# Attention and token routing in one kernel: the planner's keys get a seeded random addition, and its account of durations and landings is set anew

## The chip, the cores and the metric

The kernel runs on one core of one Trainium2 chip. The metric is device time in microseconds (us); less is better. A core has TensorE (PE in the profile; its weight loads are PEld), VectorE (DVE), ScalarE (ACT), GpSimd (POOL) and SyncE (SP), which here only issues DMA transfers. Each engine takes its instructions strictly in the order in which the program holds them. So the order of each queue is part of the program, and it is all that this change alters.

## The reference

Two stages, one after the other, all in float32:

```python
# attention: q, k, v of shape (8 batches, 8 heads, 576 tokens, 64)
q_rot, k_rot = rotate(q), rotate(k)                 # rotary embedding
scores = (1 / sqrt(64)) * q_rot @ k_rot.T
attn = exp(scores - max(scores)); attn /= sum(attn) + 1e-9
x = (attn @ v).transpose(0, 2, 1, 3).reshape(8, 576, 512)
# routing, for each batch: the 128 tokens with the highest x . w_gate
xe = x[b, top_idx]
ye = max(xe @ w1, 0) @ w2                           # 512 -> 1024 -> 512
x[b, top_idx] += sigmoid(score)[:, None] * ye
```

## The kernel before, in words

**Tiling.** Two heads of a batch form a pair; there are 32 pairs, four to a batch. A pair's queries are cut into nine units: units 0 to 7 are 128 queries of one head, unit 8 holds the last 64 of both heads.

**A pair, step by step** (lines of the kernel before). SP loads k, q and v from DRAM (L438). POOL rotates k and q (L456). PE turns them (L518), ACT and POOL split each into a high and a low part (L529 to L533, for small pieces L538 to L542). PE makes the scores (L610): twelve matmuls for two units at once (units 0 and 1, 2 and 3, 4 and 5, 6 and 7), six for unit 8; this is a score group. Each unit's scores fill two of the eight PSUM banks, so one score group of two units holds four. DVE takes the negative maximum of each unit (L627), ACT the exponential and the sum (L631); when ACT has read a unit, its banks are free. DVE then transposes the exponentials in blocks of 32x32 into the tiles `pt` (L645), and SP moves rows of `pt` from partitions to partitions (L658), six transfers for part 0 (units 0 to 3; tile pt_96) and six for part 1 (units 4 to 8; tile pt_97). The first four of six wait for the transposes alone; the last two overwrite what the first two read, and so also wait for these to land. Then PE multiplies by v (L687, the value product; 36 matmuls in the program, 72 records in the trace; it holds two banks), ACT or DVE copies the result out (L334, L336), PE turns it back and takes the gate's dot products (L731, L732; one bank), and DVE scales it (L742 to L754). After every second pair SP stores half the rows of the batch (L794, L796).

**Routing.** When a batch has its four pairs, DVE counts ranks and selects 128 tokens (L809 to L899), POOL gathers them by an indirect DMA (L906), PE runs the two layers (L924 to L971, the products are L952), and POOL scatters the rows back (L991). The weights are loaded, split and stored during the first pairs (L1014 to L1018), through two staging tiles, with POOL taking part in each of the sixteen pieces.

**What sets the order.** The kernel's code records operations (`op`) with the engine, a duration, a key, the operations that must come first, and the PSUM banks. `Order.run` then plays the whole program in its own account of time: whenever an engine is free, it takes the ready operation with the lowest key, with exceptions for score groups (`urgent`), for PE's change of tile shape (`TURN`) and for operations that would block an urgent one. Keys are due times: pair `pi` owns the stretch from `20000 * pi` on. An operation's account holds two numbers, how long its engine is taken and after how long its result is there. SP's transfers are put one after the other at 3.6 ns per KB. Where PE would idle, a filler matmul (L345) is put in, if PE was busy less than `warm` of the last stretch of the account. The list that comes out is the program; on the chip nothing is reordered.

## Time and profile before

| | us |
|---|---|
| three runs | 674.64, 681.92, 679.69 |
| median | 679.69 |
| the profiled execution, as a run | 676.31 |
| its span, first to last instruction | 674.6 |
| PE, DVE, POOL, ACT busy | 585.3, 543.9, 424.4, 361.9 |
| PE filler matmuls (L345) | 35.2 |
| granted TensorE clock, mean | 0.976 |

The profiled execution lies 1.7 us above its own span and 3.4 us under the median of the three runs. Busy times are sums over the whole span; a stage can have another limit than the mean. A wait is idle time of the engine just before an instruction, put down to whatever came last.

### The profile page before, as it was taken

Reading aid. Unit: us, or ns where it says so; the run is one execution under the profiler, and the core shown is the slowest. Engines: PE = TensorE matmul, PEld = TensorE weight load, DVE = VectorE, ACT = ScalarE, POOL = GpSimd, SP = SyncE. Lnnn points to the kernel's source line nnn. Section 1 sums busy time; section 2 is a strip of 40 time slices with the busy share of each in tenths; the row PEclk is TensorE's granted clock in tenths of the full one; section 3 lists DMA queues with packets and bytes.
Section 4 is the critical chain, followed back from the end, with each engine's and each line's share of the span. In section 5 each row is a group of like instructions: output and inputs, shape, how many; then the busy total and the mean of one; then the engine's idle time right before and its main releaser. Section 6 shows DMA issues by size and latency. Waiting matters only on the chain.

```text
span 674.6 us, 20156 instructions
## 1 busy us (share of the span) xinstructions
PE 585.3 (87%) x7828; PEld 492.9 (73%) x7828; DVE 543.9 (81%) x1348; ACT 361.9 (54%) x960; POOL 424.4 (63%) x489
## 2 busy tenths in 40 slices
PE   3787788688999988899899897989888898999997
PEld 2666667577877777788777776768777787777875
DVE  6777678868899987998889888898889878997451
ACT  2566656436666655466655556375555456554111
POOL 2989889955877565677694498475794487510101
PEclk9889999989999999899999999999999899989999
DMA  5677888748776766766785779757685776646400
GB/s 203 153 204 205 254 230 225 178 117 231 200 216 175 211 191 205 194 190 180 202 233 126 213 195 240 179 149 189 177 232 143 208 192 182 168 107 164 133 17 32
DMA packets 45951, 122.14 MB, mean 181 GB/s; under 512 B 8864, under 2 KB 18080, under 8 KB 45856
## 3 DMA queue, kind: packets, MB, share of 16 engines
q1 hardware_dynamic: 44432, 116.17, 63.6%
q0 software_dynamic: 1280, 4.20, 2.1%
q8 instruction: 62, 1.02, 0.7%
q10 hardware_dynamic: 144, 0.49, 0.2%
q14 instruction: 33, 0.27, 0.1%
HBM read 45.58 MB, written 11.53 MB: 85 GB/s over the span
## 4 chain that ended last, share of the span: by engine, by line
PE 39%; DVE 19%; DMA 16%; issue 8%; POOL 7%; ACT 7%; SPq 3%; POOLq 0%; DVEq 0%; ACTq 0%
PE ps L687 16%; DMA pt<-pt 10%; DVE pt L645 8%; PE ps L610 7%; DVE nm L627 6%; PE ps L952 6%; ACT pab L631 4%; PE ps L518 3%; SPq L658 3%; DMA xe<-w_dram 3%; PE ps L731 2%; DMA xe<-out_dram,idx 2%; PE ps L345 2%; POOL w L1018 1%; POOL m L456 1%
## 5 line engine op out<-in xcount | busy, mean ns | idle before, releaser
L631 ACT ACTIVATE pab<-ps,nm 128x576 f32<-128x576 f32 x256 | 187.1, 738 | 116.2 <-DVE nm L627 115.9
L627 DVE TENSOR_REDUCE nm<-ps 128x1 f32<-128x576 f32 x288 | 200.8, 737 | 20.2 <-PE ps L610 19.1
L645 DVE STREAM_TRANSPOSE pt<-pab 128x576 f32<-128x576 f32 x256 | 185.2, 751 | 36.0 <-PE ps L687 17.8
L687 PE MATMUL ps<-pt,vt 64*64 64x128 f32 (+1 forms) x4608 | 189.6, 300 | 25.2 <-DMA pt<-pt 8.8
L687 PEld LDWEIGHTS ps<-pt,vt 64*64 64x64 f32 x4608 | 164.7, 139 | 46.1 <-ACT pab L631 14.8
L610 PE MATMUL ps<-kh,qh 64*128 64x288 f32 (+1 forms) x576 | 88.0, 343 | 6.1 <-ACT pab L631 5.0
L456 POOL TENSOR_TENSOR rk<-k_in,m 128x512 f32<-128x512 f32 (+1 forms) x62 | 52.7, 867 | 58.8 <-PE ps L518 58.5
L610 PEld LDWEIGHTS ps<-kh,qh 64*128 64x128 f32 (+1 forms) x576 | 52.9, 192 | 34.7 <-issue 17.8
L610 PE MATMUL ps<-kh,ql 64*128 64x288 f32 (+1 forms) x576 | 72.0, 298 | 0.9 <-POOL ql L533 0.9
L456 POOL TENSOR_TENSOR rq<-q_in,m 64x64 f32<-64x64 f32 (+1 forms) x93 | 58.0, 637 | 23.4 <-PE ps L518 18.0
L533 POOL TENSOR_TENSOR kl<-xf,kh 128x512 fp32r<-128x512 f32 x31 | 39.6, 1278 | 52.3 <-ACT xf L531 38.8
L610 PE MATMUL ps<-kl,qh 64*128 64x288 f32 (+1 forms) x576 | 71.9, 297 | 0.0
L731 PE MATMUL ps<-ident,ot 128*128 128x128 f32 x160 | 47.2, 308 | 25.9 <-ACT pab L631 24.5
L334 ACT COPY ot<-ps 64x64 f32<-64x64 f32 (+1 forms) x114 | 29.0, 282 | 74.5 <-PE ps L687 73.5
L456 POOL TENSOR_TENSOR m<-k_in,tabs 128x320 f32<-128x320 f32 x62 | 52.7, 867 | 14.0 <-DVE rq L456 12.5
L731 PEld LDWEIGHTS ps<-ident,ot 128*128 128x128 f32 x160 | 30.5, 190 | 35.3 <-ACT pab L631 29.9
L610 PEld LDWEIGHTS ps<-kh,ql 64*128 64x128 f32 (+1 forms) x576 | 54.7, 191 | 1.1 <-POOL ql L533 1.1
L610 PEld LDWEIGHTS ps<-kl,qh 64*128 64x128 f32 (+1 forms) x576 | 55.0, 191 | 0.0
L952 PE MATMUL ps<-w,ht 128*128 128x512 f32 x192 | 52.7, 410 | 0.6 <-ACT pab L631 0.3
L952 PE MATMUL ps<-w,xt 128*128 128x512 f32 x192 | 52.1, 412 | 0.0
L631 ACT ACTIVATION_READ_ACCUMULATOR pab<-ps,nm 128x1 f32 x256 | 51.1, 199 | 0.0
L732 PEld LDWEIGHTS ps<-wg,ot 128*128 128x128 f32 x320 | 49.1, 209 | 1.1
(105 smaller groups left out, 923.1 us busy)
## 6 DMA issues: line engine op xcount, KB each, us to landing
pt<-pt SPq DMA_DIRECT2D x192, 180.0 KB, 3.7
pt<-pt SPq DMA_DIRECT2D x192, 144.0 KB, 3.6
vt<-v_dram SPq DMA_DIRECT2D x32, 576.0 KB, 4.9
k_in<-k_dram SPq DMA_DIRECT2D x32, 320.0 KB, 5.1
q_in<-q_dram SPq DMA_DIRECT2D x32, 288.0 KB, 4.9
out_dram<-x SPq DMA_DIRECT2D x16, 512.0 KB, 3.4
xe<-w_dram SPq DMA_DIRECT2D x8, 256.0 KB, 3.8
row<-w_dram SPq DMA_DIRECT2D x8, 256.0 KB, 4.1
```

What stands on the lines that cost most here:

```text
L334: nc.scalar.copy(out, in_)
L456: lambda: e.tensor_tensor(out, in0, in1, op=alu), key, after)
L518: nc.tensor.transpose(bank_of(b)[:, i * P:i * P + P], r.tile[:, t].rearrange("p h d -> p (h d)"), ident)
L533: d = op({"POOL": pool(n)}, lambda: nc.gpsimd.tensor_tensor(lo, xf.tile, hi.bitcast(F32), op=ALU.subtract), key, [c, y] + lu.before)
L610: nc.tensor.matmul(bank_of(bs[i])[:, n, 0:HALF], lt, rt, start=first, stop=last)
L627: lambda: nc.vector.tensor_reduce(nm.tile[:, u:u + 1], bank_of(b)[:, :, 0:HALF], axis=AX.XY, op=ALU.max, negate=True),
L631: lambda: nc.scalar.activation(dst.rearrange("p (n c) -> p n c", n=2), bank_of(b)[:, :, 0:HALF], AF.Exp, bias=nm.tile[:, u:u + 1], scale=1 ...
L645: lambda: nc.vector.transpose(pt[c].tile[:, 0:2, :, to, :].rearrange("p w m j -> p m w j"), src.rearrange("p (m w j) -> p m w j", w=2, j=32)),
L687: nc.tensor.matmul(bank_of(acc)[64 * h:64 * h + 64, g, :].rearrange("p (w c) -> p w c", w=2)[:, :, c0:c0 + n], vt.tile[gp_, h, m % 2 * NT ...
L731: nc.tensor.transpose(bank_of(b)[:, i * P:i * P + P], cols, ident)
L732: nc.tensor.matmul(bank_of(b)[:, 400 + 2 * i:402 + 2 * i], cols, wg[:, j, :], start=True, stop=True)
L952: nc.tensor.matmul(bank_of(bank), lhs.tile[:, a, c * P:c * P + P], w[w_][:, c, fs], start=(c == 0 and i == 0), stop=(c == n - 1 and i == 2))
```

## The change

It alters what the planner is told and the keys, and no operation. (1) Every key in a stretch of 20000 whose entry in `SEEDS` is not 0 gets a normally distributed addition with a standard deviation of 400, drawn from a generator with that seed. (2) Durations in the account: POOL's operations, the SP loads and stores (a load's result is now there after 4200 instead of 2000), the value product of part 1 (326 for each step instead of 283), the turning back with the gate (295 for each turned block instead of 169), the splits of the gate's scores. (3) Landings: a transfer that is issued while an earlier load has not landed is taken to land only with that load, or 2500 after it, whichever is sooner. (4) `warm` goes from 0.75 to 0.78.

```diff
@@ -1,3 +1,4 @@
+import random
 from contextlib import ExitStack
 
 import concourse.bass as bass
@@ -20,9 +21,14 @@
 EPS = 1e-9
 
 
-KEY = dict(landing=2500, warm=0.75, warm0=20000, warm1=1000000, dummy=430, dcols=256, ahead=8500, lag=13000, rem=400, value=4300, rows=3000, load=22300, rotate=115700, half=2500,
+KEY = dict(landing=2500, warm=0.78, warm0=20000, warm1=1000000, dummy=430, dcols=256, ahead=8500, lag=13000, rem=400, value=4300, rows=3000, load=22300, rotate=115700, half=2500,
            gate=11700, route=58400, count=35500, select=12400, turn=17500, step=7600, kstep=2700, hold=3,
            patience=900, over=300, near=-300, swap=6000, vsplit=9, vstep=0, recip=6000, pool_lo=1, esplit=2, s_pairs=(0, 1, 2, 3), t_banks=(2, 3, 4, 5, 6, 7), t_most=4)
+
+
+SEEDS = (395, 668, 0, 37, 0, 386, 92, 332, 986, 288, 947, 432, 0, 151, 886, 935, 438, 375, 753, 239, 325, 690, 0, 636, 130, 791,
+         968, 161, 387, 940, 0, 423, 25)
+NOISE = 400.0
 
 
 class Bank:
@@ -44,7 +50,7 @@
     SEM = 45.0
     BLOCK, FETCH = 256, 3900.0
     WINDOW, FALL, RISE = 3413.0, 0.58, 0.88
-    PER_KB = 3.6
+    PER_KB, BEHIND = 3.6, 2500.0
 
 
     TURN = {(0, 1): 97.0, (1, 0): 92.0, (0, 2): 187.0, (2, 0): 89.0, (1, 2): 187.0, (2, 1): 97.0,
@@ -93,7 +99,7 @@
                 takes -= step / (2 if slow else 1)
                 at_ += step
             return at_ - begin
-        count, fetched, moving = 0, 0.0, 0.0
+        count, fetched, moving, landing = 0, 0.0, 0.0, 0.0
         waiting = {e: [] for e in names}
         idle = [0.0] * (2 * self.pairs)
         held = {}
@@ -214,6 +220,10 @@
                     if e == "SP":
                         moving = max(moving, begin + takes) + self.PER_KB * o.size
                         begin += max(0.0, moving - begin - takes)
+                        if o.mode:
+                            landing = begin + lasts
+                        elif begin < landing:
+                            lasts = max(lasts, min(landing - begin, self.BEHIND))
                     for b in o.banks:
                         if b.slot is None:
                             b.slot = take(b.kind)
@@ -321,13 +331,13 @@
         return {"ACT": act(n), "DVE": dve(n)}
 
     def pool(n):
-        return (60 + 2.38 * n, 60 + 2.38 * n)
+        return (max(388, 60 + 2.29 * n), max(410, 100 + 2.29 * n))
 
     def pe(ns):
         return {"PE": (ns, ns + 165)}
 
     T32, T32R, M288, M512 = 109.0, 84.0, 132.5, 248.0
-    LOAD, STORE = {"SP": (500, 2000)}, {"SP": (600, 2000)}
+    LOAD, STORE = {"SP": (520, 4200)}, {"SP": (620, 2700)}
 
     def copy(e, out, in_):
         if e == "ACT":
@@ -436,7 +446,7 @@
         for i, (n, src, use) in enumerate((("k", k, kin), ("q", q, qin), ("v", v, vt))):
             if n in names:
                 o = op(LOAD, lambda src=src, use=use: nc.sync.dma_start(use.tile, src[b, j]), key + i,
-                       use.before + list(after), size=320)
+                       use.before + list(after), mode=1, size=320)
                 use.by(o)
                 got[n].append(o)
 
@@ -693,7 +703,7 @@
             o = None
             for m0 in range(0, NB // 2, KEY["vsplit"]):
                 m1 = min(m0 + KEY["vsplit"], NB // 2)
-                o = op(pe((m1 - m0) * (228 + 55 * c)), lambda m0=m0, m1=m1: products(m0, m1), key,
+                o = op(pe((m1 - m0) * (216 + 110 * c)), lambda m0=m0, m1=m1: products(m0, m1), key,
                        moved[c] + got["v"] + [o], acc, mode=1, size=16 * (m1 - m0))
                 key += KEY["vstep"]
             for use in (vt, pt[c]):
@@ -735,7 +745,7 @@
                 xrows[b_, j // 2] = xs.next()
             x = xrows[b_, j // 2]
             cs = slice(j % 2 * P, j % 2 * P + P)
-            f = op(pe((2 + c) * (T32 + 60)), turns, key, [es] + const_ready, b, size=6 * (2 + c))
+            f = op(pe((2 + c) * 295), turns, key, [es] + const_ready, b, size=6 * (2 + c))
             ot.by(f)
 
             def rows_of():
@@ -863,7 +873,7 @@
             nc.gpsimd.tensor_copy(cols[1], r1.tile)
             nc.gpsimd.tensor_tensor(cols[2], r1.tile, cols[1], op=ALU.subtract)
 
-        o = op({"POOL": (500, 500)}, parts, key, [s] + tk.before + r1.before)
+        o = op({"POOL": (1050, 1050)}, parts, key, [s] + tk.before + r1.before)
         sc.by(o), tk.by(o), r1.by(o)
         return tk, o
 
@@ -1011,8 +1021,8 @@
             st = stages.next()
             stage = st.tile
             key = at(1 + i // 4, 0.2 * (i % 4))
-            l = op(LOAD, lambda src=src, stage=stage: nc.sync.dma_start(stage, src), key,
-                   st.before + [anchors[i % 4 - 5]], size=256)
+            l = op({"SP": (520, 2900)}, lambda src=src, stage=stage: nc.sync.dma_start(stage, src), key,
+                   st.before + [anchors[i % 4 - 5]], mode=1, size=256)
             c = op({"ACT": act(DM)}, lambda hi=hi, stage=stage: nc.scalar.copy(hi, stage), key + 3000, [l])
             d = op({"POOL": pool(DM)},
                    lambda hi=hi, lo=lo, stage=stage: nc.gpsimd.tensor_tensor(
@@ -1052,6 +1062,11 @@
                 for l in held:
                     l(anchors[-KEY["hold"]:-KEY["hold"] + 1])
                 held.clear()
+    draws = [random.Random(1000 * i + n) for i, n in enumerate(SEEDS)]
+    for o in order.ops:
+        i = min(max(int(o.key // PAIR), 0), len(SEEDS) - 1)
+        if SEEDS[i]:
+            o.key += draws[i].gauss(0, NOISE)
     for _, _, o, e in order.run():
         o.fn(e) if len(o.engines) > 1 else o.fn()
```

The program that comes out has the same instructions but for one more filler matmul (67 instead of 66 in the program, two records each in the trace) and one copy that passes from DVE to ACT. The queues' order differs widely.

In the following rows kh, kl, qh, ql are the split keys and queries of a score group, ot the output of a value product, pt and vt the exponentials and v. The change's line numbers are higher by 10 (L620 is L610 of before).

**PE, around the value product of part 0 of pair 19.** Before:

```order
L687 MATMUL ps<-pt_96,vt_90 64x2x64 x36
L610 MATMUL ps<-kh_81,qh_85 128x288 x4
L610 MATMUL ps<-kl_83,qh_85 128x288 x4
L610 MATMUL ps<-kh_81,ql_87 128x288 x4
L610 MATMUL ps<-kh_81,qh_85 128x288 x4
L610 MATMUL ps<-kl_83,qh_85 128x288 x4
L610 MATMUL ps<-kh_81,ql_87 128x288 x4
L731 MATMUL ps<-ident,ot_98 128x128
```

With the change:

```order
L697 MATMUL ps<-pt_96,vt_90 64x2x64 x36
L528 MATMUL ps<-ident,rk_79 128x128 x4
L620 MATMUL ps<-kh_81,qh_85 128x288 x4
L620 MATMUL ps<-kl_83,qh_85 128x288 x4
L620 MATMUL ps<-kh_81,ql_87 128x288 x4
L741 MATMUL ps<-ident,ot_98 128x128
```

Two score groups stood back to back ahead of the turning back; now one stands there, and the turning of the next pair's keys ahead of it. Over the whole program, the turning back follows on two score groups of two units in a row 23 times before and 14 times now, on two and unit 8's between or behind them 3 and 3 times, and on a single one 17 and 32 times.

**SP, around the moves of part 0 of pair 22.** Before:

```order
L438 DMA k_in_76<-k_dram 128x640
L658 DMA pt_96<-pt_96 32x1152
L438 DMA vt_90<-v_dram 128x1152
L658 DMA pt_96<-pt_96 32x1152 x4
L438 DMA q_in_74<-q_dram 128x576
L658 DMA pt_96<-pt_96 32x1152
```

With the change:

```order
L448 DMA k_in_76<-k_dram 128x640
L668 DMA pt_97<-pt_97 32x1440 x2
L668 DMA pt_96<-pt_96 32x1152 x4
L448 DMA q_in_74<-q_dram 128x576
L668 DMA pt_96<-pt_96 32x1152 x2
L448 DMA vt_90<-v_dram 128x1152
```

The load of v stood between the first move and the next four; now it stands behind all six. Over the 32 pairs, the first four moves of part 0 have a load among them in 13 pairs before and in 5 now (pairs 0 to 3 and 17). Inside the six moves of part 1 there are 7 loads before and 15 now.

**PE, between the last value product and the last experts' first product** (sc is a batch's gate scores, xe the gathered rows, xt these turned). Before:

```order
L731 MATMUL ps<-ident,ot_99 128x128
L732 MATMUL ps<-wg,ot_99 128x2
L345 MATMUL ps<-tabs,ident 128x256 x3
L814 MATMUL ps<-ident,sc_117 128x128 x5
L924 MATMUL ps<-ident,xe_116 128x128 x4
L345 MATMUL ps<-tabs,ident 128x256 x4
L952 MATMUL ps<-w_0_131,xt_113 128x512
```

With the change:

```order
L741 MATMUL ps<-ident,ot_99 128x128
L742 MATMUL ps<-wg,ot_99 128x2
L934 MATMUL ps<-ident,xe_116 128x128 x4
L355 MATMUL ps<-tabs,ident 128x256 x2
L824 MATMUL ps<-ident,sc_117 128x128 x5
L962 MATMUL ps<-w_0_131,xt_113 128x512
```

The turning of the gathered rows comes ahead of the gate scores now, and two filler matmuls stand where seven stood.

## Rows read from the trace of the kernel before

**Rows 1.** The page: span, busy time and share by engine, the chain's shares.
```profile
span 674.6 us, 20156 instructions
...
PE 585.3 (87%) x7828; PEld 492.9 (73%) x7828; DVE 543.9 (81%) x1348; ACT 361.9 (54%) x960; POOL 424.4 (63%) x489
...
PE 39%; DVE 19%; DMA 16%; issue 8%; POOL 7%; ACT 7%; SPq 3%; POOLq 0%; DVEq 0%; ACTq 0%
```

**Rows 2.** Stages: stretch, length, busy us by engine, granted clock, DMA share, GB/s.
```profile
20.00:140.00 120.00, 93.78 (x1293) 80.20 (x1293) 87.22 (x206) 68.02 (x175) 109.64 (x117) 0.93 0.77 210
140.00:369.00 229.00, 208.65 (x2991) 176.03 (x2988) 204.50 (x484) 135.66 (x368) 152.47 (x174) 0.99 0.70 192
446.00:523.00 77.00, 69.03 (x979) 58.21 (x976) 67.27 (x166) 44.57 (x121) 52.51 (x60) 1.00 0.72 191
```

**Rows 3.** Groups by line: busy us, mean ns of one, idle before, its releasers.
```profile
L687 PE MATMUL ps<-pt,vt 64*64 64x128 f32 (+1 forms) x4608 | 189.6, 300 | 25.2 <-DMA pt<-pt 8.8 <-ACT pab L631 7.3 <-ACT h L967 2.5
L731 PE MATMUL ps<-ident,ot 128*128 128x128 f32 x160 | 47.2, 308 | 25.9 <-ACT pab L631 24.5 <-ACT ot L334 1.4
L345 PE MATMUL ps<-tabs,ident 128*128 128x256 f32 x132 | 35.2, 390 | 1.2 <-ACT xf L531 0.6 <-ACT pab L631 0.6
```

**Rows 4.** Waits over the span: who waited for whom, us, times, longest.
```profile
ACT pab L631 <- DVE nm L627: 115.9, 78, 3.3
PE ps L731 <- ACT pab L631: 24.5, 23, 1.7
PEld ps L610 <- issue: 17.8, 73, 0.4
```

**Rows 5.** Timeline, end of two score groups and the turning back of pair 19.
```profile
399.65 0.43 PE L610 MATMUL ps<-kh,ql 64*128 64x288 f32 x4
400.24 0.74 ACT L631 ACTIVATE pab<-ps,nm 128x576 f32<-128x576 f32 x1 [1.69 <-DVE nm L627]
400.98 0.73 ACT L631 ACTIVATE pab<-ps,nm 128x576 f32<-128x576 f32 x1
401.13 0.33 PE L731 MATMUL ps<-ident,ot 128*128 128x128 f32 x1 [1.05 <-ACT pab L631]
```

**Rows 6.** The chain of waits at pair 22: start, us, what.
```profile
446.58 5.42 DMA pt<-pt
...
452.08 3.18 DMA pt<-pt
```

**Rows 7.** Timeline, part 0 of pair 22, and value products of pairs 24 and 25.
```profile
445.96 0.57 SPq L438 DMA_DIRECT2D vt<-v_dram  x1
446.58 2.42 SPq L658 DMA_DIRECT2D pt<-pt  x4
...
454.20 0.43 PE L687 MATMUL ps<-pt,vt 64*64 64x128 f32 x2 [1.45 <-ACT pab L631]
455.31 1.96 PE L687 MATMUL ps<-pt,vt 64*64 64x128 f32 x61 [0.68 <-DMA pt<-pt]
...
492.35 2.35 PE L687 MATMUL ps<-pt,vt 64*64 64x128 f32 x72 [0.63 <-DMA pt<-pt]
...
510.57 1.62 PE L687 MATMUL ps<-pt,vt 64*64 64x128 f32 x42 [0.78 <-ACT h L967]
```

**Rows 8.** The page, DMA issues: count, KB each, us to landing.
```profile
vt<-v_dram SPq DMA_DIRECT2D x32, 576.0 KB, 4.9
```

**Rows 9.** Timeline of PE, from the last value product to the experts.
```profile
632.55 3.22 PE L687 MATMUL ps<-pt,vt 64*64 64x192 f32 x72
...
639.52 1.89 PE L345 MATMUL ps<-tabs,ident 128*128 128x256 f32 x8
641.06 1.25 PE L952 MATMUL ps<-w,xt 128*128 128x512 f32 x3
```

**Rows 10.** What SP's queue waited for before loads: us, times, longest.
```profile
SPq L438 <- POOL rk L456: 45.5, 14, 5.7
SPq L438 <- POOL rq L456: 28.5, 20, 3.3
```

## The prediction, made before the result

> **What bounds the kernel.** I read the page first, then the stages, then who waits. The page [rows 1]: PE is busy for 87% of the span and DVE for 81%, and the chain that ended last runs over PE for 39%, over DVE for 19%, over landings for 16%. No engine fills the span; they take turns in holding each other up. The stages [rows 2] tell three cases apart. From 20 to 140 us POOL is busy 109.64 of 120 us, since it also splits the weights, and the granted clock is 0.93. From 140 us on POOL has room, and PE and DVE share the load: in a batch of 77 us in the middle PE is busy 69.03 and DVE 67.27. So the change, which leaves the work alone, can win only PE's and DVE's idle time: about 8 and 10 us of 77 there.
>
> Where does PE wait? By line [rows 3], before the turning back (L731) 25.9 us, of which 24.5 are put down to ACT's exponential, and before the value products (L687) 25.2 us, of which 8.8 to a landing of the moves and 7.3 to the exponential. That is 51 of the 89 us in which PE is idle. The list of waits [rows 4] says that the 24.5 us are 23 waits, so 1.07 us each. The timeline shows what one is [rows 5]: two score groups end on PE at about 400.1, they hold all eight banks, the first group's second exponential begins at 400.24 and PE gets its bank at 401.13, after 1.05 us. This is a wait for PSUM: two score groups back to back and then anything that needs a bank. The order agrees: 23 is also the number of places where exactly two groups of two units stand ahead of the turning back, and the 23 waits fall on these.
>
> The other wait is a landing. In the chain at pair 22 [rows 6] the four moves that were issued behind a load of v take from 446.58 to 452.0, 5.42 us; the last move, with nothing new ahead of it, takes 3.18. The load stands between the moves because SP issues in its written order [rows 7]; the value product then waits 1.45 and 0.68 us, 2.13 together. Pair 25, with a load among its first four moves too, waits 0.78; pair 24, without one, 0.63.
>
> **The change, part by part.** No instruction is taken away. One filler matmul is added (35.2 us / 66 = 0.53 us [rows 3]) and one copy passes from DVE to ACT: nothing, as long as the filler stands where PE would wait. Nine more fillers than before now stand ahead of the seventh pair's first value product (34 against 25), in the stage that POOL limits, where PE idles 26 of 120 us [rows 2]; that idle time hides them. Without that cover they cost 9 x 0.53 = 4.8 us.
>
> Bank waits: 14 places with two score groups ahead of the turning back instead of 23. Nine fewer at 1.07 us is -9.6 us of PE waiting. Bounds: 0 if the bank is late wherever the turning back stands, and -24.5 if all go. I take -9.6, because the 17 places of before with a single group ahead of it show no such wait, and the 32 places now are like them: 30 of them have 2.75 us or more of other PE work between the two groups, as all 17 had (my sum of the durations of what stands between).
>
> Landings: a load stands among the first four moves in 5 pairs instead of 13. By rows 7, a pair with one waits (2.13 + 0.78) / 2 = 1.46, one without 0.63, so 8 x 0.83 = -6.6 us. The value products also stand further behind: with trace durations for what lies between, the PE work from the last score group of a part to its product is an estimated 16.2 us on average instead of 14.0 for part 1, 15.0 instead of 14.3 for part 0. I take -8.8, all that the rows name as a landing's; bounds 0 and -25.2, everything ahead of L687.
>
> What the load costs the moves behind it is also in the notes. The Trainium skill, DMA: Bandwidth & Descriptors, section Anatomy of one DMA, fits a DMA's time as a fixed 2.0 us and the bytes over 436 GB/s (for transfers that GpSimd issues); a v load of 576 KB [rows 8] would then hold up what is behind it by an estimated 1.35 us, not by the 5.42 - 3.18 = 2.24 us of the trace. By that rule the landing term would shrink to -5.3 us and the forecast rise by 2 us, to 669; I go by the trace, which shows this very queue.
>
> Against this stand changes of PE's tile shape: the order has 273 instead of 250 (between 64x64, 64x128 and 128x128). The nearest row is the weight loads' idle time that nobody else explains, 17.8 us in 73 cases ahead of the scores [rows 4], 0.24 each. 23 x 0.24 = +5.6 us; bounds 0, since much of it may lie under a running matmul, and 5.6. I take all of it.
>
> The tail: after the last value product PE runs fillers while it waits for the gathered rows, and the last run, 1.89 us [rows 9], stands directly ahead of the experts, after which PE works almost without a break to the end. In the new order the gathered rows are turned earlier and two fillers are left of seven. I take -1.9 us; bounds 0, if the gather lands late anyway, and 0.53 x 5 = -2.7.
>
> The noise by itself has no price: it shows in these counts. What goes from POOL's and SP's accounts into the order is in them too.
>
> The sum: -9.6 - 8.8 + 5.6 = -12.8 us of PE waiting. Not all of it reaches the end. The chain runs over PE, landings and SP's queue for 39 + 16 + 3 = 58% of the span [rows 1]; elsewhere DVE, POOL or ACT sets the pace, and a wait that PE loses there comes back at the next place. So -12.8 x 0.58 = -7.4, and the tail in full: -9.3. From the profiled execution's 676.3 this gives **667 us**. That execution lies 3.4 us under the median of the runs, 679.7; I take that as scatter between runs, and forecast 667 for the median too. Within 1%, which is about what a measurement of this kernel can tell from no change, is 672.9 to 686.5.
>
> **The rivals.**
> - *The waits turn into DVE's.* Each bank comes free only after DVE's maximum, and ACT waits 115.9 us for it [rows 4]. If DVE's queue sets the pace, the turning back simply waits in another place. For it: DVE's 67 of 77 us. Against it: PE is as busy, and DVE has 10 us of idle time in that stage. Only the tail is left, and the fillers may cost: 674 to 679, so 676.
> - *The planner wins much more.* If all bank waits and all waits before the value products go and the shape changes cost nothing: (24.5 + 25.2) x 0.58 + 1.9 = 31, so 646. For it: the account now holds the landing that it lacked. Against it: POOL limits the first stage, and 14 double groups remain.
> - *SP's queue holds the moves up: slower.* A load waits in SP's queue until POOL has finished with its tile: 45.5 + 28.5 us in 34 waits, 2.2 us each, at most 5.7 [rows 10]. Behind it the moves wait. Inside the moves of part 1 there are 15 loads now instead of 7. Each of 8 would cost 2.2 us of waiting and 2.24 of landing, 35.5 together; the 2.2 us that part 1's products stand further behind cover 17.6. The rest and the shape changes, (17.9 + 5.6) x 0.58 = 13.6 us, and none of the gains: 690. It decides from the point where a load ahead of a move waits for more than its product's slack. Against it: ahead of the first four moves of part 1 there is only one of the 15 loads (2 before), the others stand ahead of the last two, which wait for a landing anyway.
> - *The change doesn't do what it says.* The account might lengthen landings and the order still put loads between the moves. The order excludes this for part 0 (13 to 5), not for part 1.
>
> **Chances.** Forecast case 0.50; much more 0.14; DVE's pace 0.22; SP's queue 0.14. Faster by over 1%: 0.50 + 0.14, with a little of the forecast case lying above 672.9 and as much of DVE's case below it: 0.64. Within 1%: 0.22. Slower by over 1%: 0.14. The range takes in DVE's case and half of the larger gain, and leaves out 0.1 at either end: 651 to 685.
>
> **What would show it.** Right: waits of L731 for the exponential at about 15 us in 14 cases; idle time before L687 near 16 us; a middle batch of 76 us or less with PE's idle time under 8; the time from the last value product to the end shorter by 2 us than 42. Wrong: the same idle sum on PE under other lines (DVE's pace), longer waits of SP before moves with part 1's products waiting for landings (SP's queue), or more unexplained idle time before weight loads than 5.6 us above before (shape changes). The forecast fails if the planner's new account is off where I can't see it: the order shows places, not times.

## The result, and the profile after

The changed kernel took **671.33 us** (median of five runs, 667.71 to 676.84) against 676.58 for the kernel before (five runs, 674.64 to 681.92): ratio 0.990, 95% interval 0.985 to 0.994. A second set of runs beside the experiments gave 669.01 against 681.10: ratio 0.978, interval 0.973 to 0.983. The ratios leave out runs of more than 1.5% above their kernel's fastest and are not quotients of the two medians, which give 0.992 and 0.982. The forecast was 667 from 676.3, a ratio of 0.986 (0.981 from the 679.7 that the prediction took for the median), and both lie between the two measured ones. That the two intervals don't meet is taken up below, under the clock.

The profiled execution of the changed kernel was the longest of its five (676.84, granted clock 0.977), and its span is that of the kernel before (674.8 us against 674.6, at clocks of 0.977 and 0.976). The rows are read line by line instead; the second set has a profile of its own (673.5 us, span 671.4, clock 0.982). So the rows show where PE's idle time went; the whole gain of the runs is in neither profile.

The page of the changed kernel, busy times and the chain of waits, answering to [rows 1]:

```profile
span 674.8 us, 20190 instructions
...
PE 593.9 (88%) x7830; PEld 493.4 (73%) x7830; DVE 544.9 (81%) x1347; ACT 362.3 (54%) x961; POOL 425.0 (63%) x489
...
PE 32%; DVE 30%; DMA 14%; issue 9%; POOL 7%; ACT 6%; SPq 1%; POOLq 0%; DVEq 0%; ACTq 0%
```

The chain now runs over DVE for 30% instead of 19%. PE's idle time is the span less its busy time: 674.8 - 593.9 = 80.9 us, 8.4 less than before. Its busy time is 8.6 more. In the second profile idle time is 8.5 less and busy time 5.3 more.

The changed kernel's stages, answering to [rows 2] (columns: busy time of PE, PEld, DVE, ACT and POOL with counts, granted clock, DMA share, GB/s):

```profile
20.00:140.00 120.00, 101.17 (x1401) 84.33 (x1401) 95.36 (x210) 76.07 (x198) 111.32 (x119) 0.97 0.80 215
140.00:369.00 229.00, 205.90 (x2903) 172.01 (x2895) 197.85 (x484) 128.29 (x347) 152.12 (x174) 0.98 0.70 190
...
446.00:523.00 77.00, 70.61 (x918) 58.78 (x912) 64.60 (x155) 43.64 (x117) 52.00 (x60) 0.96 0.68 185
```

The first stage got 8 us more of DVE's work into the same 120 us, at a clock of 0.97 instead of 0.93 (5 us more in the second profile); the middle gave most of it back. A batch in the middle is hardly shorter: from the first value product of the second batch to that of the seventh the timelines give 380.4 us before, 383.8 with the change and 379.5 in its second profile, so 76.1, 76.8 and 75.9 us for each of the five.

PE by line in the changed kernel, answering to [rows 3] (L697 is the value product, L620 the score group, L741 the turning back, L355 the fillers; all these lines stand 10 further down than before):

```profile
L697 PE MATMUL ps<-pt,vt 64*64 64x128 f32 (+1 forms) x4608 | 186.6, 298 | 23.6 <-DMA pt<-pt 10.7 <-issue 7.2 <-ACT pab L641 4.4
L620 PE MATMUL ps<-kh,qh 64*128 64x288 f32 (+1 forms) x576 | 92.1, 348 | 9.8 <-ACT pab L641 8.0 <-ACT pr L641 1.4
...
L741 PE MATMUL ps<-ident,ot 128*128 128x128 f32 x160 | 47.6, 310 | 16.6 <-ACT pab L641 13.6 <-ACT ot L344 2.0 <-issue 0.9
...
L355 PE MATMUL ps<-tabs,ident 128*128 128x256 f32 x134 | 37.4, 404 | 3.8 <-ACT xf L541 1.8 <-ACT pab L641 1.1 <-ACT qh L539 0.7
```

The score group's line of before, which [rows 3] leaves out:

```profile
L610 PE MATMUL ps<-kh,qh 64*128 64x288 f32 (+1 forms) x576 | 88.0, 343 | 6.1 <-ACT pab L631 5.0 <-DVE ql L542 0.7
```

The list of PE's waits in the changed kernel, answering to [rows 4] (total, times, longest), and three more lines of the list of before:

```profile
PE ps L741 <- ACT pab L641: 13.6, 13, 1.6
PE ps L697 <- DMA pt<-pt: 10.7, 11, 3.2
...
PE ps L620 <- ACT pab L641: 8.0, 14, 1.4
PE ps L697 <- issue: 7.2, 7, 2.3
```

```profile
PE ps L687 <- DMA pt<-pt: 8.8, 9, 3.9
...
PE ps L610 <- ACT pab L631: 5.0, 6, 1.4
...
PE ps L687 <- issue: 0.9, 3, 0.5
```

The waits of the turning back are 13 instead of 23, at 1.05 us each, as forecast. A part came back elsewhere: the score groups wait for the exponential 8.0 us instead of 5.0, and the idle time before their first product is 9.8 instead of 6.1. The waits for landings did not go: 8.8 us in 9 cases became 10.7 in 11. The value products also wait 7.2 us, instead of 0.9, for nothing that the profile names (issue).

### The profile page after: what moved, and what is told of

It reads as the page before. It is cut to its first block, busy times and chain, and to the rows that moved or that the text cites. A ratio compares the mean times of both kernels' runs of the same rounds, so it can differ in the third digit from the quotient of the medians.

```text
span 674.8 us, 20190 instructions
## 1 busy us (share of the span) xinstructions
PE 593.9 (88%) x7830; PEld 493.4 (73%) x7830; DVE 544.9 (81%) x1347; ACT 362.3 (54%) x961; POOL 425.0 (63%) x489
## 4 chain that ended last, share of the span: by engine, by line
PE 32%; DVE 30%; DMA 14%; issue 9%; POOL 7%; ACT 6%; SPq 1%; POOLq 0%; DVEq 0%; ACTq 0%
PE ps L697 15%; DVE pt L655 12%; DMA pt<-pt 11%; DVE nm L637 10%; PE ps L620 6%; ACT pab L641 4%; PE ps L962 4%; PE ps L528 3%; DVE junk L843 2%; POOL m L466 2%; PE ps L741 2%; SPq L668 1%; PE ps L355 1%; DVE x L752 1%; DMA xe<-out_dram,idx 1%
## 5 line engine op out<-in xcount | busy, mean ns | idle before, releaser
L697 PE MATMUL ps<-pt,vt 64*64 64x128 f32 (+1 forms) x4608 | 186.6, 298 | 23.6 <-DMA pt<-pt 10.7
L697 PEld LDWEIGHTS ps<-pt,vt 64*64 64x64 f32 x4608 | 162.7, 138 | 41.8 <-issue 14.2
L620 PE MATMUL ps<-kh,qh 64*128 64x288 f32 (+1 forms) x576 | 92.1, 348 | 9.8 <-ACT pab L641 8.0
L466 POOL TENSOR_TENSOR rk<-k_in,m 128x128 f32<-128x128 f32 (+1 forms) x62 | 52.7, 867 | 59.1 <-PE ps L528 58.4
L620 PEld LDWEIGHTS ps<-kh,qh 64*128 64x128 f32 (+1 forms) x576 | 54.0, 192 | 45.2 <-issue 18.4
L620 PE MATMUL ps<-kh,ql 64*128 64x288 f32 (+1 forms) x576 | 72.8, 298 | 0.0
L620 PE MATMUL ps<-kl,qh 64*128 64x288 f32 (+1 forms) x576 | 72.5, 296 | 0.0
L741 PE MATMUL ps<-ident,ot 128*128 128x128 f32 x160 | 47.6, 310 | 16.6 <-ACT pab L641 13.6
L620 PEld LDWEIGHTS ps<-kh,ql 64*128 64x128 f32 (+1 forms) x576 | 55.4, 190 | 0.3 <-issue 0.2
L620 PEld LDWEIGHTS ps<-kl,qh 64*128 64x128 f32 (+1 forms) x576 | 55.4, 191 | 0.0
L962 PE MATMUL ps<-w,ht 128*128 128x512 f32 x192 | 51.2, 407 | 0.6 <-DVE gp L764 0.4
L742 PEld LDWEIGHTS ps<-wg,ot 128*128 128x128 f32 x320 | 49.4, 210 | 0.9
L466 POOL TENSOR_TENSOR m<-q_in,tabs 128x288 f32<-128x288 f32 x62 | 49.0, 800 | 1.3
```

The lines of the kernel that those rows point to most:

```text
L466: lambda: e.tensor_tensor(out, in0, in1, op=alu), key, after)
L620: nc.tensor.matmul(bank_of(bs[i])[:, n, 0:HALF], lt, rt, start=first, stop=last)
L697: nc.tensor.matmul(bank_of(acc)[64 * h:64 * h + 64, g, :].rearrange("p (w c) -> p w c", w=2)[:, :, c0:c0 + n], vt.tile[gp_, h, m % 2 * NT ...
L741: nc.tensor.transpose(bank_of(b)[:, i * P:i * P + P], cols, ident)
L742: nc.tensor.matmul(bank_of(b)[:, 400 + 2 * i:402 + 2 * i], cols, wg[:, j, :], start=True, stop=True)
L962: nc.tensor.matmul(bank_of(bank), lhs.tile[:, a, c * P:c * P + P], w[w_][:, c, fs], start=(c == 0 and i == 0), stop=(c == n - 1 and i == 2))
```

## The experiments

Twelve kernels (number 6 is the change once more), in three sets on three different chips, each set timed beside the kernel before: numbers 1 to 4 are the first set, 5 to 8 the second, 9 to 12 the third. The ratios of different sets are compared with that in mind. The table collects what the orders say and what was measured. "Places" are those where exactly two groups of two units stand straight ahead of the turning back; "account" is the time at which the planner's own account ends, which comes out of the kernel's code and is no measurement; (old) marks the old account, (half) half of the new one, (held) the new one with the rules of kernel 12.

| kernel | account | places | waits of the turning back for exp: cases, us | idle before value products | fillers | PE idle | ratio, 95% interval |
|---|---|---|---|---|---|---|---|
| before | 653.6 (old) | 23 | 23, 24.5 | 25.2 | 66 | 89.3 | 1 |
| the change | 647.2 | 14 | 13, 13.6 | 23.6 | 67 | 80.9 | 0.990 (0.985-0.994) |
| the change again | 647.2 | 14 | 14, 14.9 | 23.3 | 67 | 80.8 | 0.978 (0.973-0.983) |
| account only | 661.0 | 23 | 23, 28.0 | 23.1 | 74 | 85.7 | 1.002 (0.997-1.006) |
| additions only | 663.2 (old) | 13 | 13, 16.3 | 25.0 | 99 | 90.4 | 1.022 (1.019-1.026) |
| other seeds | 684.6 | 16 | 17, 20.6 | 38.1 | 91 | 101.5 | 1.040 (1.035-1.045) |
| before, loads behind | 653.6 (old) | 23 | 22, 31.7 | 14.8 | 66 | 89.5 | 0.992 (0.989-0.996) |
| change, loads behind | 647.2 | 14 | 14, 14.7 | 9.0 | 67 | 71.8 | 0.969 (0.965-0.974) |
| drawn for old account | 637.8 (old) | 21 | 21, 24.3 | 27.4 | 64 | 95.0 | 0.999 (0.996-1.003) |
| more drawn | 644.9 | 14 | 15, 15.9 | 27.6 | 58 | 84.3 | 0.985 (0.980-0.991) |
| drawn afresh | 642.5 | 14 | 14, 15.9 | 21.7 | 61 | 75.3 | 0.986 (0.981-0.992) |
| old products, drawn | 642.3 (half) | 18 | 18, 24.4 | 26.8 | 72 | 87.1 | 0.999 (0.996-1.003) |
| old loads, drawn | 644.4 (half) | 16 | 16, 19.4 | 29.5 | 58 | 88.8 | 1.000 (0.996-1.004) |
| loads held, drawn | 645.0 (held) | 16 | 15, 17.0 | 18.9 | 56 | 75.3 | 0.971 (0.966-0.976) |

**1. The account alone.**

```diff
-        if SEEDS[i]:
+        if False:
```

> The new durations and warm as in the change, no random addition (every seed taken as 0). In its order PE has 23 places with two score groups straight ahead of the turning back, as before (14 with the change), and one load of v among the first four moves of part 0 (13 before, 2 with the change). Bank theory (the gain is bank waits that the additions broke up): about 676, no different from before, with the waits of the turning back for the exponential at 20 us or more. Account theory (the new durations carry the gain, the additions are decoration): 671, ratio 0.99. Landing theory (loads among the moves carry it): 671 too, but then with the idle time before the value products under 20 us instead of 25.2.

Measured: 1.002, no gain (the median of all twelve runs, 685.14, lies 0.5% above before's); 23 places and 23 waits. The new durations, with `warm` at its new value, do nothing alone. No run has `warm` by itself. The landing theory falls too as an account of the whole: the order has 34 loads between the moves instead of 44, its landing waits are 6.2 us instead of 8.8, and it wins nothing. (Its profiled execution had a clock of 0.958 and a span of 688.5, long against its own median; its counts are read here, not its totals.)

**2. The additions alone**, on the old account: before's code with `SEEDS`, `NOISE` and the loop that draws.

> The random additions with the same seeds on the old account (old durations, warm 0.75). 13 places with two score groups straight ahead of the turning back. Bank theory: 671, like the change, and turning back waits for the exponential about 14 us. Account theory: 676 or more, since the additions only disturb the order. Chosen-seeds theory (the seeds help only with the account that they were drawn for): 676 to 682.

Measured: 1.022, slower. The bank theory falls here as an account of the whole: this order has the fewest places of all, 13, its waits of the turning back are down to 16.3 us, and it loses 2%. PE's list of lines of this kernel shows where the time is:

```profile
L352 PE MATMUL ps<-tabs,ident 128*128 128x256 f32 x198 | 54.1, 409 | 2.8 <-ACT pab L638 1.7 <-ACT xf L538 1.1
```

99 fillers instead of 66, 54.1 us instead of 35.2. A filler is written where the planner itself sees PE with nothing to do; so the additions pushed work apart, and the idle time is in the order as fillers, not as waits. That the fillers only fill this time and don't cost any of their own was not tested.

**3. Another draw of the same size.**

```diff
-    draws = [random.Random(1000 * i + n) for i, n in enumerate(SEEDS)]
+    draws = [random.Random(1000 * i + n + 1) for i, n in enumerate(SEEDS)]
```

> The change with every generator started from the next seed, so another draw of the same size for the same stretches. 16 places with two score groups straight ahead of the turning back, 6 loads of v among the first four moves of part 0. Bank theory: 672 to 673, since 7 of the 9 places are gone. Chosen-seeds theory: 675 to 682, whatever the count of places. Account theory: 671.

Measured: 1.040, the slowest of all, though 16 places stand in its order. In its profile 49.4 us are fillers, and the value products wait longer:

```profile
L697 PE MATMUL ps<-pt,vt 64*64 64x128 f32 (+1 forms) x4608 | 193.4, 306 | 38.1 <-DMA pt<-pt 16.3 <-ACT pab L641 10.1 <-issue 5.7
```

So the two draws that were not selected on the account they ran with lost 2.2% and 4.0%, and it is the choice of the seeds that pays. Two draws don't say what a draw costs on average.

**4 and 5. Loads behind the moves.** SP's queue alone is altered: after the planner has run, each load of q, k, v or weights between the six moves of a part is put behind the sixth (42 of 44 loads in the kernel before, 43 of 48 in the change; the others stay between the moves). The function that does it is left out here.

```diff
-    for _, _, o, e in order.run():
+    plan = [(o, e) for _, _, o, e in order.run()]
...
+    for o, e in behind(plan):
```

> The kernel before, with SP's queue alone altered: every load of q, k, v or weights that stands between the six moves of a part is issued behind the sixth (42 loads; no other engine's order changes). Landing theory as the prediction priced it (8.8 us of landing waits before the value products, 58% of it reaching the end): 671, ratio 0.992. Rival, a landing is hidden or waits turn into others of the same size: 676, ratio 1.00, even if the idle time before the value products falls. Second rival, the loads come too late for the rotation: over 680.

> The change with SP's queue alone altered: each load that stands between the six moves of a part is issued behind the sixth. Landing theory (a load of any kind ahead of any of the six moves delays the value product; 10.7 us of landing waits are left with the change): the landing waits go to about 0 and the ratio falls by 0.006 to 0.980 to 0.984. Rival (the change already took the harmful loads, those of v among the first four moves, 13 to 2, so there is nothing left to win): 0.990. Second rival (DVE's pace): the landing waits go and the turning back waits as much longer: 0.990.

Measured: 0.992 on the kernel before, as the landing theory said; 0.969 on the change, against 0.978 for the change in the same set, so 0.991 again (the two intervals, 0.965 to 0.974 and 0.973 to 0.983, just touch; the medians, 660.87 and 669.01, give 0.988). In the second 5.8 us of landing waits were left; I had expected about none. The value products' and the turning back's lines of before with its loads behind, then the value products' line of the change with its loads behind:

```profile
L687 PE MATMUL ps<-pt,vt 64*64 64x128 f32 (+1 forms) x4608 | 185.7, 297 | 14.8 <-ACT pab L631 10.8 <-ACT pr L631 1.3 <-DVE gg L899 0.9
...
L731 PE MATMUL ps<-ident,ot 128*128 128x128 f32 x160 | 47.8, 311 | 33.5 <-ACT pab L631 31.7 <-ACT ot L334 1.8
```

```profile
L697 PE MATMUL ps<-pt,vt 64*64 64x128 f32 (+1 forms) x4608 | 179.8, 293 | 9.0 <-DMA pt<-pt 5.8 <-ACT pab L641 1.9 <-ACT xt L937 0.9
```

Idle time before the value products fell by 10.4 us in the one and by 14.3 in the other, and 0.8% and 0.9% of the time, some 5 to 6 us each (8 by the medians of the second), reached the end: a share of 0.4 to 0.6. In the first the turning back took 7.6 us of it (33.5 us of idle time instead of 25.9), so the DVE's-pace rival holds in part there; PE's idle time as a whole is no less in that profile (89.5 us against 89.3), so what the 0.8% is made of is not shown. In the second it is 71.8 against 80.8. The waits put down to nothing went with the loads as well, from 7.6 us in the second profile of the change to 0.2; that they were waits for landings too is likely and not shown. The timeline shows one case. SP's queue in the changed kernel, then PE there:

```profile
401.61 3.83 SPq L668 DMA_DIRECT2D pt<-pt  x4
405.54 0.53 SPq L448 DMA_DIRECT2D vt<-v_dram  x1
406.55 1.48 SPq L668 DMA_DIRECT2D pt<-pt  x2
```

```profile
412.63 3.86 PE L697 MATMUL ps<-pt,vt 64*64 64x128 f32 x72 [3.21 <-DMA pt<-pt]
```

The load of v stands ahead of the *last two* moves, which the prediction held to be harmless, and the product waits 3.21 us. The same place with the load behind, SP and PE:

```profile
396.68 6.27 SPq L668 DMA_DIRECT2D pt<-pt  x6
403.04 0.53 SPq L448 DMA_DIRECT2D vt<-v_dram  x1
```

```profile
405.44 0.40 PE L697 MATMUL ps<-pt,vt 64*64 64x128 f32 x2 [0.97 <-DMA pt<-pt]
406.16 2.19 PE L697 MATMUL ps<-pt,vt 64*64 64x128 f32 x70 [0.32 <-DMA pt<-pt]
```

0.97 and 0.32 us are left. The product itself takes 3.86 us in the one and 0.40 + 2.19 in the other. The granted clock goes with this; the stretch of the changed kernel around the product:

```profile
410.00:420.00 10.00, 6.38 (x103) 5.93 (x103) 5.78 (x12) 3.97 (x10) 7.37 (x8) 0.83 0.55 162
```

Microsecond by microsecond the clock is 1.00 up to 412, while PE waits, and 0.50 from 413 to 415, during the product; with the load behind, the row from 400 to 410 has 1.00. So the wait was followed by a fall of the clock, with which the product took 1.3 us more; this part of the price shows as busy time, not as a wait. Over the whole program the value products' busy time fell from 184.6 to 179.8 us with the loads behind the moves.

From the end of the last issue to the last landing that PE waited for it was 412.63 - 408.03 = 4.60 us with the load ahead and 406.16 - 402.95 = 3.21 without, so the load cost 1.39 us here, where [rows 6] gave 2.24. By the Trainium skill, DMA: Bandwidth & Descriptors, section Anatomy of one DMA, the part of a DMA's time that grows with its size is the bytes over 436 GB/s (a fit for transfers that GpSimd issues): an estimated 1.35 us for a load of this size. This place agrees with it, the other does not.

**6. The change once more.**

> The change itself once more, for its ratio beside the other runs of this call and for a second profile. Ratio 0.990 again, with waits of the turning back for the exponential near 14 us. If the first ratio was scatter of the clock: 1.00.

Measured: 0.978. Its lines agree with those of the first profile: 14.9 us in 14 waits of the turning back, 23.3 us before the value products. The gain is no scatter.

**7. Seeds drawn for the old account**: kernel 2 with seeds chosen by replacing one or two at a time and keeping what lets the planner's account end earlier.

> The old account (old durations, warm 0.75) with random additions of the same size from seeds that were drawn for it, by how early the planner's account ends: 637.8 us of the account instead of 653.6 without additions. The order has 21 places with two score groups straight ahead of the turning back (23 before, 14 with the change) and 5 loads of v among the first four moves of part 0. Theory of the draw (any shortening of the account by selected seeds passes on to the chip at about 0.6): 15.8 x 0.6 = -9.5 us, ratio 0.986. Rival (the new durations make the account true enough to choose by; selection on the old one fits its errors): 1.00 or above. Bank theory: 2 places fewer at 1.07 us, ratio 0.998.

Measured: 0.999. The account fell by 15.8 us and the chip saw nothing. What was won on the old account was its errors.

**8 and 9. Seeds drawn for the new account**: the change with 12 seeds replaced, and with all drawn anew from none, chosen in the same way.

> The change with 12 of its 33 seeds replaced, so that the planner's account ends at 644.9 us instead of 647.2 (without additions 661.0, with the next seeds 684.6). Theory of the draw: -2.3 x 0.6 = -1.4 us against the change, ratio 0.987 to 0.989. Rival (the seeds of the change were chosen by times on the chip, which the account does not know): like another draw, 1.00 or above.

> The change with all 33 seeds drawn anew, from none, by how early the planner's new account ends: 642.5 us (647.2 with the seeds of the change, 661.0 without additions). Theory (seeds selected on the new account pay, 0.9 us on the chip for one of the account between the runs so far): -18 x 0.9 = -16 us against the account alone, ratio 0.976. Rival (the seeds of the change were picked by times on the chip as well, the account alone can't do it): 0.995 to 1.005.

Measured: 0.985 and 0.986. Choosing by the account alone does it, without times from the chip; but the second gave -10 us, not the -16 that I expected, and an account shorter by 2.3 or 4.7 us than the change's is no faster. Among these three orders the account tells nothing more.

**10 and 11. Half the new account**, with seeds drawn for each: with PE's two old durations, and with the old ones of POOL, loads and stores.

```diff
-                o = op(pe((m1 - m0) * (216 + 110 * c)), lambda m0=m0, m1=m1: products(m0, m1), key,
+                o = op(pe((m1 - m0) * (228 + 55 * c)), lambda m0=m0, m1=m1: products(m0, m1), key,
...
-            f = op(pe((2 + c) * 295), turns, key, [es] + const_ready, b, size=6 * (2 + c))
+            f = op(pe((2 + c) * (T32 + 60)), turns, key, [es] + const_ready, b, size=6 * (2 + c))
```

> The change's account, but with PE's two old durations (value product of part 1 at 283 a step instead of 326, a turned block at 169 instead of 295), and seeds drawn for that account, which ends at 642.3. If PE's two durations make the account true: 1.00, like the seeds drawn for the whole old account. If they don't matter: 0.976 to 0.985, like seeds drawn for the new one.

> The change's account, but with the old durations of POOL's operations and of SP's loads and stores (a load there after 2000 instead of 4200), and seeds drawn for that account, which ends at 644.4. If these durations make the account true: 1.00. If they don't matter: 0.976 to 0.985. Nine loads of v stand among the first four moves of part 0 (2 with the change), so landing waits should be above 12 us.

Measured: 0.999 and 1.000. With either half of the account as it was, the selected seeds win nothing. It is one set of seeds for each account; a second one was not drawn. Their orders show why in part: 18 and 16 places, and 26.8 and 29.5 us before the value products; but kernel 8 has 27.6 us there and is faster. In the second the landing waits were 11.8 us; I had expected more than 12.

**12. Loads held by the planner, seeds drawn for it.** The planner doesn't start a load while a part's moves are under way, and a move behind a load is counted to land with it.

```diff
+                        if e == "SP" and o.mode and steps % 6:
+                            put.append(item)
+                            continue
                         can, new = o.ready, {}
...
+                        steps += o.size in (144, 180)
```

> The change with a planner that doesn't start a load of q, k, v or weights between the six moves of a part and counts moves behind a load under way as landing with it (up to 5500 instead of 2500), and seeds drawn for that account, which ends at 645.0. If the two gains add (selected seeds on a true account, no load between moves): 0.965 to 0.970, landing waits under 6 us, and at or under the change with its loads issued behind the moves (0.969). Rival (what the additions win is what the held loads win): 0.980.

Measured: 0.971, as good as the change with loads behind the moves (0.969) and no better; 8.0 us of landing waits were left, more than the 6 that I expected. The first was timed beside the change, and the second was not. These two are the fastest kernels here: 660.87 us against 681.10, and 660.82 against 679.52.

## Why the prediction was right, and where it was not

- **Bank waits, right.** -9.6 us was forecast; the idle time before the turning back fell by 9.3 us (15.7 are left in the second profile: by 10.2). The reading behind it, that each place with two score groups ahead of the turning back is one wait of about 1.07 us, held in every order: places and waits differ by one at most in all fourteen rows of the table, at 1.0 to 1.4 us each, and in both profiles of the change each of the 13 and 14 waits falls on such a place. But 3.7 us of it came back before the score groups (9.8 us of idle time instead of 6.1), as the rival of DVE's pace said.
- **Landings, wrong.** -8.8 us was forecast, to about 16 us before the value products; -1.6 and -1.9 came. The step that failed is "a load stands among the first four moves in 5 pairs instead of 13", taken for the whole: a load ahead of the last two moves holds them as well (the case above), and 44 loads between moves had become 48. The price was misread too: 1.46 us for a pair with a load and 0.63 for one without were taken from waits of which [rows 7] put only 0.68 and 0.63 down to a landing, and 1.45 and 0.78 to ACT. With the waits put down to nothing, the price of landings may even have risen, from 9.7 us to 17.9. The mechanism is real (kernels 4 and 5), only the change doesn't use it. Nor does its landing rule do anything: a move's own landing is 2500 in the account, `BEHIND` is 2500 too, and the order of all five queues is the same with the rule taken out. That was to be read from the diff; the rival that the change doesn't do what it says had it half right.
- **Tile shapes, over-priced and under another name.** +5.6 us of idle time was forecast; the unexplained idle time before the scores' weight loads went from 17.8 to 18.7 (second profile 19.8). PE's *busy* time in the first product of a score group rose instead, from 88.0 to 92.1 (second profile 92.4). One step of it, in the second profile of the change:

```profile
403.75 0.53 PE L620 MATMUL ps<-kh,qh 64*128 64x288 f32 x4
404.12 0.42 PE L620 MATMUL ps<-kl,qh 64*128 64x288 f32 x4
404.39 0.42 PE L620 MATMUL ps<-kh,ql 64*128 64x288 f32 x4
404.65 0.43 PE L620 MATMUL ps<-kh,qh 64*128 64x288 f32 x4
404.91 0.42 PE L620 MATMUL ps<-kl,qh 64*128 64x288 f32 x4
```

  Behind other work the first product takes 0.53 us and the next starts 0.37 later; directly behind a score group 0.43 and 0.26. With 35 score groups directly behind another before and 27 now that makes about 1 us; where the rest of the 4 comes from I haven't found.
- **The tail, not shown.** -1.9 us was forecast for the time from the last value product to the end; 42.05 us [rows 9] became 674.8 - 633.82 = 40.98, -1.1. Two fillers (four records) are left behind the gathered rows, and the experts begin 640.30 - 633.82 = 6.48 us behind the product instead of 8.51; of these 2.0 us, 1.0 is lost further on:

```profile
633.82 3.28 PE L697 MATMUL ps<-pt,vt 64*64 64x192 f32 x72
...
638.50 0.63 PE L934 MATMUL ps<-ident,xe 128*128 128x128 f32 x4
638.97 1.03 PE L355 MATMUL ps<-tabs,ident 128*128 128x256 f32 x4
639.84 0.71 PE L824 MATMUL ps<-ident,sc 128*128 128x128 f32 x5
640.30 5.85 PE L962 MATMUL ps<-w,xt 128*128 128x512 f32 x24
```

  In the second profile the same order has no gain: 671.4 - 628.61 = 42.79 us, 0.7 more than before. The value product takes longer there, and the gathered rows come late, which is the bound of 0 that the prediction gave:

```profile
628.61 3.79 PE L697 MATMUL ps<-pt,vt 64*64 64x192 f32 x72 [0.18 <-DMA pt<-pt]
...
634.98 0.66 PE L934 MATMUL ps<-ident,xe 128*128 128x128 f32 x4 [1.04 <-DMA xe<-out_dram,idx]
```

- **The sum, right, and largely by luck.** Of -9.6 - 8.8 + 5.6 = -12.8 us the first came nearly in full, the second hardly and the third as other work; idle time fell by 8.4 us and busy time rose by as much. The share of 0.58 that reaches the end measured 0.4 to 0.6 for landings. The middle batch was to be 76 us or less with PE idle for under 8: PE's idle time came (6.4 us of 77), the shorter batch did not (76.8 and 75.9 us against 76.1). The forecast had no term for the clock, with which much of the gain goes (last section). So the time came out in the forecast's place, and not by the forecast's path.
- **SP's queue, excluded.** The rival's waits went the other way: SP's waits for POOL ahead of loads, 74.0 us in [rows 10], are

```profile
SPq L448 <- POOL rq L466: 33.2, 15, 6.5
...
SPq L448 <- POOL rk L466: 11.8, 7, 4.8
```

  45.0 now.
- **"The noise by itself has no price", the deeper miss.** True of this order, and no reason: another draw of the same size is 4% slower than before. How the seeds of the change were found isn't known. What the runs show is that selection pays on the new account and not on the old one or on half of the new one (three sets of seeds against three: kernels 6, 8, 9 and 7, 10, 11). The account's error shows the same: the median on the chip is longer than the account by 23 to 28 us for the kernel before, by 22 to 29 for all five kernels of the new account, but by 42 for the seeds drawn on the old one (34 for kernel 2, which has the old one and seeds that weren't drawn on it) and by 38 and 35 for those on half. Selecting there found orders that the account has wrong. Not every new duration is nearer to the trace: a load's landing is (2.0 before, 4.2 now, medians of 4.9 to 5.1 us in the trace of before), a turned block is (0.17, 0.295, 0.29), but POOL's operation on 512 columns was nearer before (1.279, 1.232, 1.279), and kernel 11 doesn't separate POOL's durations from the loads'. I read the order that came out and could price it; I didn't see that the two parts of the change are worth nothing apart.

## What to carry to other kernels

Selecting among random schedules paid here only where the model that selects had been corrected: first set the durations from the trace, then draw, and stop when the model's gain no longer shows on the chip. Random additions that were not selected on the model they ran with lost 2.2% and 4.0% here. A transfer that something waits for soon should not stand behind a large load in the same queue, not even its last piece: moving the loads alone, with nothing else changed, won 0.8 to 0.9% in two different orders. And when two kernels differ by about 1%, list the clock of their runs beside the times.

## What the runs showed of the hardware

The granted clock goes with the time from run to run. The change's eleven runs had a mean clock of 0.977 to 0.993 (median 0.987) and took 676.84 to 662.25 us; the kernel before, in the three sets of experiments, had 0.960 to 0.981 (median 0.970). At 0.976 to 0.978 the change's one run took 676.84 and six of the kernel before 675.32 to 679.57; at 0.980 to 0.982 three of the change took 670.63 to 673.51 and two of before 678.04 and 679.37. So much of the change's gain, and the difference between its two ratios, goes together with time at 1.2 instead of 2.4 GHz. An estimate from the means: at 0.970 of 679 us some 41 us were spent at the low level, at 0.987 of 669 us some 17; at half the clock PE loses at most half of such time, 12 us of the difference. Another, by straight lines through the runs: 0.01 of clock goes with 3.8 us in the 59 runs of the kernel before and with 7.1 us in the eleven of the change, so the 0.017 between the medians goes with 6 to 12 us, against a gain of 5 to 12 us by the medians of the two sets. At an equal clock these lines leave the change between nothing and about half of its gain, the five runs at 0.980 to 0.982 some 7 us. Whether the clock made the change faster or a smoother order the clock higher was not separated: no run held one of them fixed. At one place, under kernels 4 and 5, the trace speaks for the second: PE waits 3.21 us, and then the clock falls. The freshly drawn seeds and the held loads gained 1.4% and 2.9% at a median clock of 0.972, against 0.971 for the kernel before in that set, so a gain of this kind doesn't need a higher clock. Nor does a higher clock make a gain: the seeds drawn for the old account had a median of 0.976 against 0.968 and a ratio of 0.999.
